# A pruned matrix product on one core: other places for the first loads, one transpose in a product bank, and another opening order on TensorE

## The chip, the core and the metric

The kernel runs on one core of a Trainium2 chip. Its engines run side by side, each with its own queue of instructions: TensorE (PE; its weight loads are shown as PEld), VectorE (DVE), ScalarE (ACT), GpSimd (POOL) and SyncE (SP), which here only issues transfers. ScalarE issues transfers too. The metric is device time in microseconds, the median of several runs.

## The reference

`x` is 16 x 512 x 1024, `w` 1024 x 1024 and `b` 1024 long, all bf16. Of every four neighbouring rows of `w`, in every column, the two of largest magnitude are kept; then a plain product and the bias:

```python
wg = w.reshape(G, M, D)                      # M = 4, G = D // 4
mag = jnp.abs(wg)
order = jnp.argsort(mag, 1)
thr = jnp.take_along_axis(mag, order[:, M - N:M - N + 1, :], 1)   # N = 2
mask = (mag >= thr).astype(w.dtype)
wp = (wg * mask).reshape(D, D)
return jnp.einsum("bsd,df->bsf", x, wp) + b
```

## The kernel before

The 8192 rows of `x` are 64 tiles of 128. From tile 12 on the kernel is a steady stream: a batch of tiles is loaded transposed by DMA (line 377), each tile takes 16 matmuls 512 wide against the pruned weights (line 239), and DVE adds the bias while it empties PSUM (line 400). All that matters here is the opening, in which the weights are still being loaded and pruned.

**Loads** (lines 110 to 124). `w` comes in pieces, the first 256 columns of its upper half in four DMAs that alternate between SyncE and ScalarE. `load_x` brings the left half of `x` for tiles 0 to 7. Each engine issues its DMAs in the order in which they are written. ScalarE's only other work at that point is a small activation (line 116), which has its table loaded.

**Pruning** (class Piece, lines 143 to 180). Six pieces of `w` are pruned one after the other, 0 to 3 of the upper half, 4 and 5 of the lower. For piece i the steps are abs, hi, lo, t1, t2, thr, mask and mult. DVE does all of them but one: the magnitudes of piece 3 (`abs3`) are made on ScalarE (line 157). Piece 0 has its mask and mult in four quarters u, v, s, t (one of the four rows of a group each), piece 1 in two halves x and y. The pruned rows stand in an interleaved order in `wp`; four DMAs a half ("W" tokens, line 141) spread them in natural order into `wp_nat`.

**Tiles 0 to 7** are multiplied in that interleaved order while pieces 0 to 3 come in. A tile t has its left half transposed by four matmuls with the identity ("T", line 189) into a bank of PSUM, and ScalarE copies it to SBUF ("C", line 194). Products "Mt.i" with a letter take the quarter or half of piece i (line 216, 256 columns, one matmul for each of the four rows of a group). Two tiles share a bank: the pairs are (5, 6), (0, 1), (2, 3), (4, 7), numbered 0 to 3. When a pair's products for a 256-column strip n are all done, ScalarE copies the bank to SBUF ("Sqbn", line 256: pair q, strip n), which frees it. So S2b0 waits for all products of piece 0 of tiles 2 and 3.

**Tiles 8 to 11** come transposed by DMA ("X" tokens, line 224); tokens "Ajhn" open their sums with the upper half (line 239), and lines 432 to 433 close them, then those of tiles 0 to 7, whose right half comes by the "Y" tokens (line 231). POOL adds the bias to the staged sums.

PSUM has eight banks: two in the pool `psum_t` (transposes, later tile 11) and six in `psum_o` (everything else, the fillers first). A tile of a pool gets a bank when the one that had it has been read.

**The order of the work is written out by hand**: lists of tokens for PE, DVE, ACT and SP (lines 258 to 280). `run` emits them engine by engine, a token as soon as what `needs` names for it has been emitted, and `seq` (line 64) ties each engine's instructions to that order. Fillers (line 133: 6 wide, 8 and then, as token F8, 8 narrow matmuls of constants) occupy TensorE while the first loads are under way. A transpose needs the copy of the one two before it, since `psum_t` has two banks.

In the order before, T7a, T5a and T6a stand first on TensorE, then products and transposes in turn, and all 32 products of piece 0 (8 tiles, u, v, s, t) precede the first of piece 1. ScalarE's list has the eight copies, S3b0, S0b0, S1b0, S2b0, then `abs3`, then further stage copies. Two of the four spreading DMAs of the lower half (W1.0q) are issued by ScalarE ahead of S3b3 and S0b3.

Of the kernel before, what the change touches and what calls it, by code (L numbers as in the profile page):

```python
# [10 lines left out]
def kernel(  # L11
# [8 lines left out]
    P = 128  # L20
    bf16 = mybir.dt.bfloat16
    fp32 = mybir.dt.float32
# [10 lines left out]
    FH = 512  # L33
# [24 lines left out]
    psum_t = ctx.enter_context(tc.tile_pool(name="psum_t", bufs=2, space=bass.MemoryType.PSUM))  # L58
    psum_o = ctx.enter_context(tc.tile_pool(name="psum_o", bufs=6, space=bass.MemoryType.PSUM))
# [10 lines left out]
    def pe(i):  # L70
        return seq("pe", i)
# [4 lines left out]
    def act(i):  # L76
        return seq("act", i)
# [13 lines left out]
    def tokens(dram, t):  # L91
        a, b_ = next(s for s in GROUPS if s[0] <= t < s[1])
        return dram[a * P:b_ * P].rearrange("(p t) k -> p t k", p=P), t - a
    bias_sb = const.tile([P, Dout], bf16)

    def issue(eng, out_, in_):
        q = nc.sync if eng == "sp" else nc.scalar
        return seq(eng, q.dma_start(out_, in_))  # L98

    def load_w(g, c0, c1, ma=0, mb=4, eng="sp"):  # L100
        issue(eng, w_sb[:, g, ma:mb, c0:c1], wv[:, g, ma:mb, c0:c1])

    def load_x(ta, tb, eng="sp"):
        xs = const.tile([P, tb - ta, HK], bf16, name=f"x_{ta}")
        xv, n = tokens(xf, ta)
        issue(eng, xs[:], xv[:, n:n + tb - ta, :HK])
        for t in range(ta, tb):
            x_sb[t] = xs[:, t - ta, :]
# [2 lines left out]
    load_w(0, 0, 256, 1, 2, "act")  # L111
    load_w(0, 0, 256, 2, 3)
    load_w(0, 0, 256, 3, 4, "act")
    load_x(7, 8, "act")
    load_x(0, 2, "act")
    act(nc.scalar.activation(spark[:], nc.const_aps.tensor(1.0, [P, 1], bf16), Act.Abs))
    load_x(5, 7)
    load_w(0, 256, 512)
    load_x(4, 5)
    load_x(2, 4)  # L120
    load_w(0, 512, 1024)
    load_w(1, 0, 512)
# [8 lines left out]
    def filler(n, rep=1):  # L131
        for _ in range(n):
            pe(nc.tensor.matmul(warm_ps[:, :rep * P], lhsT=nc.const_aps.tensor(1.0, [P, P], bf16),  # L133
                                rhs=nc.const_aps.tensor(1.0, [P, rep * P], bf16), start=True, stop=True))
# [4 lines left out]
    def spread(g, c0, c1, ks=range(4), eng="sp"):  # L139
        for k in ks:  # L140
            issue(eng, wp_nat[:, 4 * g + k, c0:c1], wp[32 * k:32 * k + 32, g, :, c0:c1])
# [41 lines left out]

    def transpose(t):
        xg = x_sb[t].rearrange("p (q m) -> p m q", m=4)
        bank = psum_t.tile([P, FH], fp32, name="tp")
        tp = bank[:].bitcast(bf16)[:, :FH].rearrange("p (m q) -> p m q", m=4)
        for m in range(4):
            pe(nc.tensor.transpose(tp[:, m, :], xg[:, m, :], ident[:]))  # L189
        xpk[t] = tp  # L190

    def copy_xt(t):
        xt = xtp.tile([P, 4, P], bf16, name="xt")
        act(nc.scalar.copy(xt[:].bitcast(fp32), xpk[t].bitcast(fp32)))  # L194
        xpk[t] = xt
# [27 lines left out]
    def load_lead(g):  # L223
        sp(nc.sync.dma_start_transpose(out=xlead[:, 4 * g:4 * g + 4, :],
                                       in_=xf[NPK * P:(NPK + LEAD) * P, g * HK:(g + 1) * HK]))
        return {NPK + j: xlead[:, :, j * P:(j + 1) * P] for j in range(LEAD)}

    def load_low(u):
        a, b_ = GROUPS[u]
        xlow = const.tile([P, 4, (b_ - a) * P], bf16, name=f"xlow{u}")  # L230
        sp(nc.sync.dma_start_transpose(out=xlow[:], in_=xf[a * P:b_ * P, HK:]))
        xq = xlow[:].rearrange("p k (q t) -> p k q t", t=b_ - a)
        return {a + t: xq[:, :, :, t] for t in range(b_ - a)}
# [8 lines left out]
    def open_nat(j, h):  # L242
        t = NPK + j
        if j < 3:
            held[(t, h)] = psum_o.tile([P, FH], fp32, name="ps")
        else:
            held[(t, h)] = psum_t.tile([P, FH], fp32, name="tp")
        nat(xnat[t], held[(t, h)][:], h * FH, (h + 1) * FH, 0, 4)
# [3 lines left out]
    def stage(q, n):  # L252
        if (q, n // 2) not in staged:
            staged[(q, n // 2)] = stg.tile([P, 2, 2, CW], fp32, name="st")
        st = staged[(q, n // 2)]
        act(nc.scalar.copy(st[:, n % 2, :, :].rearrange("p t c -> p (t c)"), ps_open.pop((q, n))[:]))  # L256

    order = {
        "pe": (
            "F8 T7a T5a T6a M7.0u M5.0u T1a M7.0v M5.0v M6.0u M6.0v T0a M7.0s M5.0s M6.0s M7.0t M5.0t M6.0t "  # L260
            "T4a M1.0u M1.0v M1.0s M1.0t T3a M0.0u M0.0v M0.0s M0.0t T2a M4.0u M4.0v M4.0s M4.0t "
            "M3.0u M3.0v M3.0s M3.0t M2.0u M2.0v M2.0s M2.0t M4.1x M5.1x M0.1x M7.1y M6.1y M2.1y M1.1y "
            "M3.1y M6.1x M4.1y M1.1x M3.1x M0.1y M7.1x M2.1x M5.1y M0.2 M3.2 M7.2 M1.2 M2.2 M4.2 "
            "M6.2 M0.3 M2.3 M5.3 M4.3 M5.2 M6.3 M3.3 M1.3 A0h0 A2h0 M7.3 A2h1 A1h0 A3h1 A0h1 A3h0 "
            "A1h1"
        ),
        "dve": (
            "abs0a hi0a abs0b lo0a lo0b hi0b t20 t10 thr0 mask0u mask0v mult0u mult0v mask0s mask0t mult0s mult0t abs1 lo1 hi1 "
# [2 lines left out]
            "thr5 mask5 mult5"  # L271
        ),
        "act": (
            "C7a C5a C6a C1a C0a C4a C3a C2a S3b0 S0b0 S1b0 S2b0 abs3 S3b1 S1b1 S0b1 S2b1 S2b2 S1b2 "
            "S3b2 S0b2 S1b3 S2b3 W1.0q S3b3 S0b3"
        ),
        "sp": (
# [9 lines left out]
    def all_of(tok, i):  # L287
        return [tok + x for x in halves.get(i, ("",))]

    def split_tok(tok):  # L290
        k = tok[-1] if tok[-1] in "xyabuvst" else ""
        return (tok[:-1] if k else tok), k

    transposed = []

    def needs(eng, tok):
        base, k = split_tok(tok)
        if tok[0] == "C":
            return ["T" + tok[1:]]
        if tok[0] == "T":  # L300
            return ["C" + transposed[-2]] if len(transposed) > 1 else []
        if tok[0] == "F":
            return []
        if tok[0] == "W":
            g, h = map(int, tok[1:4].split("."))
            return [n for i, pc in enumerate(pieces) if pc[0] == g and pc[1] // FH == h for n in all_of(f"mult{i}", i)]
        if tok[0] in "XY":
            return []
        if tok[0] == "A":
            return ["X0", f"W0.{tok.split('h')[1]}"]  # L310
        if base[0] == "M":
            t, i = base[1:].split(".")
            return [f"C{t}a", f"mult{i}{k}"]
        if tok[0] == "S":
            q, n = map(int, tok[1:].split("b"))
            return [f"M{t}.{x}" for i, pc in enumerate(pieces) if pc[0] == 0 and pc[1] // CW == n
                    for t in pairs[q] for x in all_of(str(i), i)]
        i, step = base[-1], base[:-1]
        before = {"abs": [], "hi": ["abs"], "lo": ["abs"], "t1": ["hi"], "t2": ["lo"],
                  "thr": ["t1", "t2"], "mask": ["thr", "hi", "lo"], "mult": ["mask"]}[step]  # L320
        out_ = []
        for b_ in before:
            if b_ in ("abs", "hi", "lo") and int(i) in by_rows:
                out_ += [b_ + i + k] if step in ("hi", "lo") else [b_ + i + s for s in "ab"]
            else:
                out_.append(b_ + i + (k if b_ == "mask" else ""))
        return out_

    def emit(eng, tok):
        base, k = split_tok(tok)  # L330
        if tok[0] == "T":
            transpose(int(tok[1:-1]))
            transposed.append(tok[1:])
        elif tok[0] == "F":
            filler(int(tok[1:]))
        elif tok[0] == "W":
            g, h = map(int, tok[1:4].split("."))
            spread(g, h * FH, (h + 1) * FH, {"": range(4), "p": range(2), "q": range(2, 4)}[tok[4:]], eng)
        elif tok[0] == "X":
            xnat.update(load_lead(int(tok[1:])))  # L340
        elif tok[0] == "Y":
            xnat.update(load_low(int(tok[1:])))
        elif tok[0] == "A":
            open_nat(*map(int, tok[1:].split("h")))
        elif tok[0] == "C":
            copy_xt(int(tok[1:-1]))
        elif tok[0] == "M":
            mm_piece(*map(int, base[1:].split(".")), part[k])
        elif tok[0] == "S":
            stage(*map(int, tok[1:].split("b")))  # L350
        else:
            i = int(base[-1])
            if i not in p:
                p[i] = Piece(i)
            if eng == "act":
                p[i].abs_act()
            else:
                p[i].do(base[:-1], part[k], half.get(k, slice(0, 2)))
# [78 lines left out]
    for bi, (tb, nb) in enumerate(batches):  # L437
        if bi:
            load_batch(bi + 1)
        for j in range(nb):  # L440
            t = tb + j
            xt = xnat[t]
            o = outp.tile([P, Dout], bf16, name="o")
            if t == NT - 1:
                for n, (c0, c1) in enumerate(((0, FH), (FH, FH + CW), (FH + CW, Dout - P), (Dout - P, Dout))):
                    ps = psum_o.tile([P, FH], fp32, name="ps")
# [44 lines left out]
```

## Time and profile before

| what | value |
|---|---|
| time, median of 3 runs | 233.24 us (233.21 to 233.59) |
| the profiled execution's own time | 233.31 us |
| its span | 231.5 us |
| first weights read by DVE (abs0a) | starts at 3.10 us |
| first transpose on TensorE | starts at 5.28 us |
| S3b0 to S2b0, first strip's stage copies | 10.31 to 12.36 us |
| abs3 on ScalarE | 12.23, 1.09 long |
| first sums of tiles 8 to 11 open | 21.03 us |
| mult5, the last step of pruning | ends at 27.66 us |
| first batch of the steady stream | TensorE from 49.1 us |

Times in the traces count from the start of the span. A line of the timeline gives start, length, engine, line of the kernel, operation, what is written from what, and in brackets how long the engine stood before it and what released it. A matmul's length includes the way through the array, so matmuls overlap; the distance between starts is what each costs in a stream.

### The profile page before, as it was taken

Reading aid. Unit: us, or ns where it says so; the run is one execution under the profiler, and the core shown is the slowest. Engines: PE = TensorE matmul, PEld = TensorE weight load, DVE = VectorE, ACT = ScalarE, POOL = GpSimd, SP = SyncE. Lnnn points to the kernel's source line nnn. Section 1 sums busy time; section 2 is a strip of 40 time slices with the busy share of each in tenths; the row PEclk is TensorE's granted clock in tenths of the full one; section 3 lists DMA queues with packets and bytes.
Section 4 is the critical chain, followed back from the end, with each engine's and each line's share of the span. In section 5 each row is a group of like instructions: output and inputs, shape, how many; then the busy total and the mean of one; then the engine's idle time right before and its main releaser. Section 6 shows DMA issues by size and latency. Waiting matters only on the chain.

```text
span 231.5 us, 2851 instructions
## 1 busy us (share of the span) xinstructions
PE 227.7 (98%) x1158; PEld 112.6 (49%) x1158; DVE 107.8 (47%) x188; ACT 13.7 (6%) x27; POOL 17.6 (8%) x15
## 2 busy tenths in 40 slices
PE   8999999999999999999999999999999999999995
PEld 5887444544444444444444444444444444444443
DVE  4999778754334324324424424424424423423434
ACT  2774100000000000000000000000000000000000
POOL 1000299700000000000000000000000000000000
DMA  6999989997299222992249921795129962122122
GB/s 198 358 216 223 223 179 256 271 258 273 94 231 262 99 91 63 224 272 80 88 119 224 246 93 59 163 283 151 73 91 181 226 182 82 57 91 86 57 87 91
DMA packets 78268, 38.19 MB, mean 165 GB/s; under 512 B 63664, under 2 KB 70576, under 8 KB 78256
## 3 DMA queue, kind: packets, MB, share of 16 engines
q1 hardware_dynamic: 67328, 20.61, 44.1%
q10 hardware_dynamic: 10928, 17.40, 21.5%
q8 instruction: 9, 0.15, 0.3%
q14 instruction: 3, 0.02, 0.0%
HBM read 3.41 MB, written 16.78 MB: 87 GB/s over the span
## 4 chain that ended last, share of the span: by engine, by line
PE 96%; DMA 2%; ACTq 0%; ACT 0%; DVE 0%; issue 0%
PE ps L239 88%; PE ps L216 6%; DMA x<-in_x_dram 2%; PE tp L239 1%; PE tp L189 1%; ACTq L98 0%; ACT xt L194 0%; DVE o L400 0%
## 5 line engine op out<-in xcount | busy, mean ns | idle before, releaser
L239 PE MATMUL ps<-wp_nat,xb 128*128 128x512 bf16 (+2 forms) x848 | 179.8, 375 | 0.0
L239 PEld LDWEIGHTS <-xb 128*128 128x128 bf16 x848 | 82.4, 98 | 97.5
L400 DVE TENSOR_TENSOR o<-ps,bias_sb 128x512 bf16<-128x512 f32 (+1 forms) x112 | 71.6, 677 | 114.4 <-PE ps L239 114.3
L396 POOL TENSOR_TENSOR st<-st,bias_sb 128x1024 f32<-128x1024 f32 x8 | 16.8, 2131 | 0.0
L216 PE MATMUL ps<-wp,xt 128*128 128x256 bf16 x128 | 15.1, 273 | 0.0
L239 PE MATMUL ps<-wp_nat,xlow 128*128 128x512 bf16 x64 | 14.1, 379 | 0.0
L216 PEld LDWEIGHTS <-xt 128*128 128x128 bf16 x128 | 12.2, 98 | 1.6
L402 DVE TENSOR_TENSOR o<-ps,st 128x512 bf16<-128x512 f32 x16 | 11.1, 692 | 2.8 <-PE ps L239 2.3
L239 PE MATMUL ps<-wp_nat,xlead 128*128 128x512 bf16 x48 | 11.2, 379 | 0.0
L239 PEld LDWEIGHTS <-xlow 128*128 128x128 bf16 x64 | 7.2, 112 | 6.7
L239 PEld LDWEIGHTS <-xlead 128*128 128x128 bf16 x64 | 6.2, 98 | 7.1
L256 ACT COPY st<-ps 128x512 f32<-128x512 f32 x16 | 8.4, 595 | 6.0 <-PE ps L216 3.7
L154 DVE TENSOR_TENSOR mag<-mag,hi 128x256 bf16<-128x256 bf16 (+3 forms) x10 | 5.6, 582 | 0.2
L154 DVE TENSOR_TENSOR wp<-w_sb,mag 128x256 bf16<-128x256 bf16 (+3 forms) x10 | 5.6, 580 | 0.1
L133 PE MATMUL ps<-const-bfloat16-1.0 128*128 128x128 bf16 (+1 forms) x22 | 4.4, 395 | 0.8 <-PEq L475 0.8
L164 DVE TENSOR_SCALAR mag<-w_sb 128x512 uint16<-128x512 uint16 (+2 forms) x6 | 2.7, 466 | 3.1 <-DMA w_sb<-in_w_dram 3.1
L239 PE MATMUL tp<-wp_nat,xlead 128*128 128x512 bf16 x16 | 4.1, 379 | 0.0
L133 PEld LDWEIGHTS <-const-bfloat16-1.0 128*128 128x128 bf16 x22 | 2.5, 143 | 2.4 <-issue 2.4
L189 PE MATMUL tp<-ident,x 128*128 128x128 bf16 x32 | 3.0, 220 | 0.3 <-ACT xt L194 0.2
L154 DVE TENSOR_TENSOR hi<-mag 128x512 bf16<-128x512 bf16 (+2 forms) x7 | 3.2, 459 | 0.1
L154 DVE TENSOR_TENSOR lo<-mag 128x512 bf16<-128x512 bf16 (+2 forms) x7 | 3.1, 457 | 0.0
L194 ACT COPY xt<-tp 128x256 f32<-128x256 f32 x8 | 2.9, 374 | 3.2 <-PE tp L189 3.1
(15 smaller groups left out, 13.5 us busy)
## 6 DMA issues: line engine op xcount, KB each, us to landing
out_dram<-o ACTq DMA_DIRECT2D x59, 256.0 KB, 2.9
wp_nat<-wp SPq DMA_DIRECT2D x14, 128.0 KB, 3.4
w_sb<-in_w_dram SPq DMA_DIRECT2D x3, 512.0 KB, 6.3
out_dram<-o ACTq DMA_DIRECT2D x8, 128.0 KB, 1.7
x<-in_x_dram SPq DMA_DIRECT2D x2, 256.0 KB, 3.9
w_sb<-in_w_dram SPq DMA_DIRECT2D x1, 256.0 KB, 4.8
x<-in_x_dram ACTq DMA_DIRECT2D x1, 256.0 KB, 3.8
bias_sb<-in_b_dram SPq DMA_DIRECT2D x1, 256.0 KB, 6.4
```

Source lines behind the costliest of these rows:

```text
L133: pe(nc.tensor.matmul(warm_ps[:, :rep * P], lhsT=nc.const_aps.tensor(1.0, [P, P], bf16), rhs=nc.const_aps.tensor(1.0, [P, rep * P], bf16), ...
L154: dve(nc.vector.tensor_tensor(out, a, b_, op=op))
L164: dve(nc.vector.tensor_single_scalar(self.mag[:, ms, :].bitcast(u16), self.w[:, ms, :].bitcast(u16), 0x7FFF, op=Alu.bitwise_and))
L189: pe(nc.tensor.transpose(tp[:, m, :], xg[:, m, :], ident[:]))
L194: act(nc.scalar.copy(xt[:].bitcast(fp32), xpk[t].bitcast(fp32)))
L216: pe(nc.tensor.matmul(ps[:, c0 + d:c1 + d], lhsT=xpk[t][:, m, :], rhs=wp[:, g, m, c0:c1], start=(new and m == ms.start), stop=(left[(q, n) ...
L239: pe(nc.tensor.matmul(ps, lhsT=xt[:, kt - koff, :], rhs=wp_nat[:, kt, c0:c1], start=(kt == first), stop=(kt == last)))
L256: act(nc.scalar.copy(st[:, n % 2, :, :].rearrange("p t c -> p (t c)"), ps_open.pop((q, n))[:]))
L396: pool(nc.gpsimd.tensor_tensor(st[:], st[:], bias[:, :, None, :].to_broadcast([P, 2, 2, CW]), op=Alu.add))
L400: dve(nc.vector.tensor_tensor(o[:, c0:c1], ps, bias_sb[:, c0:c1], op=Alu.add))
L402: dve(nc.vector.tensor_tensor(o[:, c0:c1].rearrange("p (n c) -> p n c", n=2), ps.rearrange("p (n c) -> p n c", n=2), add, op=Alu.add))
```

## The change

Three things, and nothing else:

- The loads: tiles 5-6 and tile 4 are issued by ScalarE, third and fourth on it, in place of tile 7 and tiles 0-1. Tile 7 is third on SyncE in place of tiles 5-6. Tiles 0-1 come on SyncE behind the second weights, in place of tile 4.
- T6a writes to a bank of `psum_o` and not of `psum_t`. It has no copy to wait for and is not counted among the transposes that later ones wait for.
- The order: T4a comes fourth and C4a fourth. The products of piece 0 are in another order, and M2.0t, the last of them, stands behind eight tokens (sixteen matmuls) of piece 1.

```diff
-    load_x(7, 8, "act")
-    load_x(0, 2, "act")
+    load_x(5, 7, "act")
+    load_x(4, 5, "act")
     act(nc.scalar.activation(spark[:], nc.const_aps.tensor(1.0, [P, 1], bf16), Act.Abs))
-    load_x(5, 7)
+    load_x(7, 8)
     load_w(0, 256, 512)
-    load_x(4, 5)
+    load_x(0, 2)
     load_x(2, 4)
...
-        bank = psum_t.tile([P, FH], fp32, name="tp")
+        bank = psum_o.tile([P, FH], fp32, name="ps") if t == 6 else psum_t.tile([P, FH], fp32, name="tp")
...
         "pe": (
-            "F8 T7a T5a T6a M7.0u M5.0u T1a M7.0v M5.0v M6.0u M6.0v T0a M7.0s M5.0s M6.0s M7.0t M5.0t M6.0t "
-            "T4a M1.0u M1.0v M1.0s M1.0t T3a M0.0u M0.0v M0.0s M0.0t T2a M4.0u M4.0v M4.0s M4.0t "
-            "M3.0u M3.0v M3.0s M3.0t M2.0u M2.0v M2.0s M2.0t M4.1x M5.1x M0.1x M7.1y M6.1y M2.1y M1.1y "
-            "M3.1y M6.1x M4.1y M1.1x M3.1x M0.1y M7.1x M2.1x M5.1y M0.2 M3.2 M7.2 M1.2 M2.2 M4.2 "
-            "M6.2 M0.3 M2.3 M5.3 M4.3 M5.2 M6.3 M3.3 M1.3 A0h0 A2h0 M7.3 A2h1 A1h0 A3h1 A0h1 A3h0 "
-            "A1h1"
+            "F8 T7a T5a T6a M7.0u T4a M7.0v M5.0u M5.0v M6.0v M6.0u M6.0s M5.0t M4.0u M5.0s M4.0s M7.0s "
+            "T1a M7.0t M6.0t M4.0v T0a M4.0t M1.0u T3a M1.0v M1.0t M0.0v M0.0t T2a M0.0s M1.0s M0.0u "
+            "M3.0u M3.0t M3.0s M2.0u M3.0v M2.0v M2.0s M7.1y M5.1x M6.1y M0.1x M4.1x M2.1y M6.1x M4.1y "
+            "M2.0t M1.1x M1.1y M3.1x M3.1y M0.1y M7.1x M2.1x M5.1y M0.2 M3.2 M7.2 M1.2 M2.2 M4.2 M6.2 "
+            "M0.3 M2.3 M5.3 M4.3 M5.2 M6.3 M3.3 M1.3 A0h0 A2h0 M7.3 A2h1 A1h0 A3h1 A0h1 A3h0 A1h1"
         ),
...
-            "C7a C5a C6a C1a C0a C4a C3a C2a S3b0 S0b0 S1b0 S2b0 abs3 S3b1 S1b1 S0b1 S2b1 S2b2 S1b2 "
+            "C7a C5a C6a C4a C1a C0a C3a C2a S3b0 S0b0 S1b0 S2b0 abs3 S3b1 S1b1 S0b1 S2b1 S2b2 S1b2 "
...
         if tok[0] == "T":
-            return ["C" + transposed[-2]] if len(transposed) > 1 else []
+            return ["C" + transposed[-2]] if tok != "T6a" and len(transposed) > 1 else []
...
             transpose(int(tok[1:-1]))
-            transposed.append(tok[1:])
+            if tok != "T6a":
+                transposed.append(tok[1:])
```

## The prediction

> **What bounds the kernel now.** I read the page's first part, then the chain of waits in order of time, then the waits of TensorE, then timelines of single engines.
>
> ```profile
> PE 227.7 (98%) x1158; PEld 112.6 (49%) x1158; DVE 107.8 (47%) x188; ACT 13.7 (6%) x27; POOL 17.6 (8%) x15
> ```
>
> TensorE is busy for 227.7 of 231.5 us. Its work is not changed in number or size, so the change can only win or lose where TensorE stands still. The chain in order of time (start, length, what) shows where that is:
>
> ```profile
> 1.66 3.57 DMA x<-in_x_dram
> 5.24 0.05 issue
> 5.28 0.43 PE tp L189 x4
> 5.71 0.02 issue
> 5.73 0.38 ACT xt L194
> 6.11 0.04 issue
> 6.16 0.38 PE tp L189 x4
> ...
> 9.84 11.35 PE ps L216 x104
> ```
>
> and the waits of TensorE in the first 60 us (who for whom, total, times, longest):
>
> ```profile
> PE ps L133 <- PEq L475: 0.8, 1, 0.8
> PE tp L189 <- ACT xt L194: 0.2, 1, 0.2
> ```
>
> Tile 7 lands at 5.24 and its transposes start at 5.28; the fillers' weight loads end at 4.93 (3.29 + 1.64 in the timeline), so 0.35 us pass there. T6a then waits for C7a: eight transposes at 0.055 each would end at 5.72, T6a starts at 6.16, 0.44 lost. After 6.16 no wait is listed; the products run at 0.109 each and the last matmul ends the kernel. **So the opening holds at most 0.35 + 0.44 = 0.79 us, 0.34% of 233.24.**
>
> The other side is how near TensorE's suppliers run behind it. Timelines of ACT, DVE and PE, in that order of fences (start, us, engine, line, op, idle before):
>
> ```profile
> 9.88 0.37 ACT L194 COPY xt<-tp 128x256 f32<-128x256 f32 x1 [0.29 <-PE tp L189]
> 10.31 2.05 ACT L256 COPY st<-ps 128x512 f32<-128x512 f32 x4
> 12.23 1.09 ACT L157 ACTIVATE mag<-w_sb 128x1024 bf16<-128x1024 bf16 x1
> ...
> 22.84 1.67 ACTq L98 DMA_DIRECT2D wp_nat<-wp  x2
> 24.55 1.07 ACT L256 COPY st<-ps 128x512 f32<-128x512 f32 x2 [2.25 <-DVE hi L154]
> ```
>
> ```profile
> 12.96 0.69 DVE L154 TENSOR_TENSOR wp<-w_sb,mag 128x1024 bf16<-128x1024 bf16 x1
> 13.57 0.41 DVE L154 TENSOR_TENSOR hi<-mag 128x512 bf16<-128x512 bf16 x1
> ```
>
> ```profile
> 24.92 1.03 PE L239 MATMUL tp<-wp_nat,xlead 128*128 128x512 bf16 x4
> 25.78 1.03 PE L239 MATMUL ps<-wp_nat,xlead 128*128 128x512 bf16 x4
> ```
>
> The reader is to see: S3b0 to S2b0 and then abs3 follow each other on ScalarE; abs3 ends at 13.32, only 0.25 before DVE's hi3 at 13.57. DVE has no gap from 3.10 to 27.66, so what is late at hi3 is late in mult3, mult4 and mult5. W1.0q (22.84) waits for mult4 and holds S3b3 (24.55) and S0b3 behind it on ScalarE; those free the banks of A0h1 (25.78) and A1h1 (27.51).
>
> **Part 1, loads.** The same bytes are moved in the same eight first DMAs, so nothing is added or removed. Tile 7 takes the place (SyncE, third, issued at 1.65) in which tiles 5-6, twice its bytes, landed at 1.65 + 3.3 = 4.95; it is there by then, and the start is set by the fillers, 4.93 to 4.95. Tiles 5-6 take ScalarE's third place: tile 7 landed from it at 5.24, tiles 0-1 from the fourth at 2.15 + 3.8 = 5.95. Both are bounds; as the queue has moved 128 KB less than for the second, I take 5.3. Tile 4 comes fourth there, with the same bytes ahead and including it as tiles 0-1 had: 5.95, wanted at 6.16. Tiles 0-1 are issued at 3.10: tile 4 landed from there at 7.2, tiles 2-3 from the next place at 8.0; both queues together have asked for 1,280 KB by its end as they had by tile 4's, so 7.2 to 7.4, wanted at 7.6. The second weights are behind 128 KB less, and DVE is busy until 6.92 anyway: no gain. Bias and the last weights go out behind as before. Four issues stand on ScalarE ahead of its table load in both versions, so that moves nothing.
>
> The Trainium skill, DMA: Bandwidth & Descriptors, section Issuing engines are not separate DMA queues, speaks against this part: loads of either engine run on the same 16 DMA engines, and a second queue saves only issue time. This trace does not quite agree: 256 KB from SyncE landed 0.3 us before 128 KB from ScalarE, issued within 0.02 us. By the rule alone tile 7 would land at 5.24 as now, and the time would be 0.1 us longer than the sum below.
>
> **Part 2, T6a in a product bank.** T7a, T5a and T6a no longer wait for a copy: from 4.95, 0.22 for each, T5a and T6a from 5.3, so they end at 5.74. M7.0u needs C7a and mult0u. C7a: tile 7's transposes to copy 0.45, copy 0.37, to TensorE 0.05 (6.10 to 6.16): 4.95 + 0.87 = 5.82. mult0u: 5.71 + 0.28 + 0.05 = 6.04, the later. Before, M7.0u stood at 6.38 with the same 12 transposes done. Gain 6.38 - 6.05 = 0.33. In the new order M5.0t then meets mult0t (6.72 + 0.28 + 0.05 = 7.06, wanted at 7.04), 0.02 lost, and no other copy or mult is late by more: M7.1y is wanted at 10.88 - 0.31 = 10.57, mult1y is there at 9.92 + 0.42 + 0.05 = 10.39. **So the gain g is 0.30.** Its lower end is -0.05 (tiles 5-6 only at 5.95: M7.0u at 6.42); the upper end 0.33. T6a's bank is one more allocation of psum_o, but it is also one more bank already free, so every later bank waits for the same copy as before.
>
> The clock: the fillers still step at 0.107 us at 4.89, the transposes at 0.055 from 5.37, so the faster step came between. Twelve transposes at 0.107 from 4.95 would end at 6.23 and take 0.18 of g away.
>
> The Trainium skill, TensorE: Matmul & The Clock Gate, section Part 1: The HAM clock gate, says the switch follows about 3.4 us of work and, its window running freely, can shift by 0.5 us. No run here shows the shift; four products of 0.109 at half speed would make the time 0.4 us longer by it.
>
> **Part 3, new opening order.** M2.0t, the last product of S2b0's bank, moves from the 32nd product to the 48th. Before, the 33rd stands at 9.68 + 12 x 0.109 = 10.99, so the 48th at 12.63 - g. ScalarE's copy starts 0.31 after its last product (M4.0t at 9.68 + 3 x 0.109 = 10.01, S3b0 at 10.31): S2b0 at 12.94 - g. Behind it on the same engine stands abs3, one copy pitch later ((12.23 - 10.31) / 4 = 0.48): 13.42 - g, ending 1.09 later at 14.51 - g, and hi3 can start at 14.56 - g where it stood at 13.57. **DVE is 0.99 - g = 0.69 us late from hi3 on.** What covers that, each cover less 0.99 since TensorE itself comes g earlier:
> - mult3 at 16.50 + 0.05, M0.3 wants it at 17.54: 0.99 of cover, just met.
> - W1.0: its last piece landed at 23.52 + 4.0 = 27.5, wanted by (8,0)'s last matmul at 29.02: 1.5, enough. W1.1: 33.7 against 35.06: 1.35, enough. Y0 behind W1.0p on SyncE lands at 31.5, wanted at 40.2.
> - W1.0q on ScalarE: S3b3 at 24.55 + 0.59 + 0.05 = 25.19, A0h1 at 25.78: **0.59 only. TensorE stands 0.99 - 0.59 = 0.40 us before A0h1.** S0b3 is wanted at 27.51 and ends at 25.63: 1.88, enough.
>
> That S3b3 and not S0b3 frees A0h1's bank I infer: both A0h1 and A1h1 wait for ScalarE again, which the second would not need if the first had waited for the later copy. The second DMA of W1.0q took 1.00 us to issue, its first 0.64; most wp_nat issues take 0.60. If 0.36 of it belongs to a transfer that no longer overlaps it, the stall is 0.04. I take its own row, 1.00.
>
> **Sum** against the profiled execution (span 231.5, 233.31 with what lies around it, 0.07 above the median 233.24): -0.30 + 0.40 = +0.10, so 233.34 from the median; its own range 232.95 to 233.6. After A0h1 no wait is listed up to the end, and the batch loads land 10 us or more before use (for the second batch 52.5 against 62.9), so this stays to the end.
>
> **Rivals.**
> 1. The opening's gain arrives whole: W1.0q's second issue takes 0.64 and the stall vanishes. For it: 13 of 16 such issues are at 0.64 or less. Against: this one's own row. 233.24 - 0.30 = 232.94.
> 2. Slower: A0h1 takes the bank that S0b3 frees. Its cover is 25.78 - 25.68 = 0.10, so TensorE stands 0.99 - 0.10 = 0.89 there: +0.59, 233.83. For it: q0's last bank was opened (M5.3) before q3's (M4.3), and a plain rotation would give it out first. Against: A1h1's own wait. The same price comes if the second issue is 1.57 long, as one of W1.1's was. It decides from a stall of 0.77 on.
> 3. The opening gives nothing, tiles 5-6 landing at 5.95: g = -0.05, the stall unchanged at 0.99 - 0.59: 233.24 + 0.05 + 0.40 = 233.69.
> 4. More than the 0.47 us of 0.2% is won: the opening's 0.79 would have to come almost whole, but mult0u at 6.04 stands in the way, unless DVE's first weights land earlier. 232.7.
>
> **How the numbers follow.** Forecast 0.42, rival 1 0.17, rival 2 0.23, rival 3 0.10, rival 4 0.08. A measurement of this kernel can tell about 0.2% (0.47 us) from no change. Forecast, rival 1 and rival 3 lie within it but for their edges: 0.02 of rival 1 is faster, 0.04 of rival 3 slower. Faster 0.10, slower 0.27, same 0.63. The range goes from rival 1 to rival 2: 232.9 to 233.85.
>
> **What would show it.** Tile 7's transposes at 4.95 and T6a without a gap; M7.0u near 6.05. S2b0 alone near 12.65 with ScalarE idle ahead of it, abs3 near 13.1; DVE idle 0.7 us ahead of hi3, released by ScalarE's line 157; TensorE idle near 25.5 for 0.4 us, released by line 256. No gap on DVE at hi3 would overturn part 3; a gap of TensorE elsewhere, above all ahead of T5a, T1a, M0.3 or (8,0), would make the prediction wrong in its working.

## The result and the profile after

The changed kernel takes 233.73 us (median of 22 runs, 233.13 to 234.21), the kernel before 233.35 us beside it (22 runs, 233.07 to 233.62). The ratio is 1.0014, 95% interval 1.0008 to 1.0021: slower by 0.33 us, 0.19 to 0.49. The prediction was 233.34, net +0.10; its range, 232.9 to 233.85, holds the time, but +0.10 lies below the interval of the difference. The profiled execution took 234.21 us, the highest of the 22, with a span of 232.4, so it shows the loss larger than the median has it.

The page's first part, the changed kernel:

```profile
PE 227.5 (98%) x1158; PEld 112.0 (48%) x1158; DVE 108.0 (46%) x188; ACT 13.5 (6%) x27; POOL 17.6 (8%) x15
```

TensorE's busy time is that of before within 0.2; the 0.9 us of span are idle time. The chain of waits in order of time (start, length, what) says where:

```profile
3.02 5.49 DMA x<-in_x_dram
8.51 0.05 issue
8.55 0.41 PE tp L189 x4
...
10.62 2.96 PE ps L216 x27
...
13.61 0.59 ACT st L256
14.19 0.97 ACT mag L157
...
15.18 0.42 DVE hi L154
...
23.21 1.22 DVE wp L154
...
25.14 0.88 ACTq L98
...
26.06 0.59 ACT st L256
...
26.69 1.02 PE ps L239 x4
```

Before, the chain ran through TensorE alone from 6.16 on. Now it begins with a load of `x` that lands at 8.51 and starts T1a (8.55). It runs through M2.0t into S2b0 (13.61) and abs3 (14.19), then through sixteen steps of VectorE from hi3 (15.18) to mult4 (23.21), W1.0q on ScalarE and S3b3 (26.06), and comes back to TensorE at A0h1, 26.69 where before had 25.78: 0.91 later. TensorE's timeline splits the 0.91:

```profile
25.59 1.03 PE L239 MATMUL tp<-wp_nat,xlead 128*128 128x512 bf16 x4
26.69 1.02 PE L239 MATMUL ps<-wp_nat,xlead 128*128 128x512 bf16 x4
```

A3h1, the group just ahead, starts at 25.59 where before had 24.92. So 0.67 was lost earlier, and 0.24 is the wait at A0h1 itself (26.69 less 25.59, less the 0.86 that the four matmuls of A3h1 take). The waits of the first 60 us, the same kernel:

```profile
PE tp L189 <- DMA x<-in_x_dram: 0.9, 1, 0.9
...
DVE hi L154 <- ACT mag L157: 0.8, 1, 0.8
PE ps L216 <- DVE wp L154: 0.6, 1, 0.6
```

The first is T1a, the second hi3, the third M7.0u on mult0u. The first transposes and T1a in TensorE's timeline:

```profile
4.56 0.62 PE L189 MATMUL tp<-ident,x 128*128 128x128 bf16 x8
5.01 0.39 PE L189 MATMUL ps<-ident,x 128*128 128x128 bf16 x4
5.97 0.27 PE L216 MATMUL ps<-wp,xt 128*128 128x256 bf16 x1 [0.56 <-DVE wp L154]
...
6.29 1.39 PE L216 MATMUL ps<-wp,xt 128*128 128x256 bf16 x11
8.55 0.41 PE L189 MATMUL tp<-ident,x 128*128 128x128 bf16 x4 [0.87 <-DMA x<-in_x_dram]
```

T7a starts at 4.56, 0.72 earlier than before, T6a follows with no gap, M7.0u starts at 5.97 where it stood at 6.38: the opening did what it was to do, 0.41 won there. The last of the eleven products ahead of T1a starts at 7.41 and takes 0.109 in the stream, so T1a starts 1.04 after TensorE was free (the bracket's 0.87 counts from that product's end): all of the 0.41 is lost again, and 0.63 more.

A second place where the two traces differ is the queue of SyncE's loads. What SyncE's queue (q1) and ScalarE's (q10) moved from 3.7 to 4.7 us (packets, MB, share of the DMA engines), before:

```profile
q10 hardware_dynamic: 250, 0.24, 77.3%
q1 hardware_dynamic: 111, 0.10, 29.9%
```

and after:

```profile
q10 hardware_dynamic: 289, 0.27, 90.5%
q1 hardware_dynamic: 12, 0.01, 9.2%
```

With tile 7 done (4.34), SyncE's queue is as good as empty for much of that microsecond although the second weights had been issued at 2.11 and 2.12. Their first packets move at 4.44 where before had 4.71, and from 4.7 to 7.2 the queue moves 0.73 MB in either kernel: having less ahead of them gains them little. Whether this hole is what made tiles 0-1 late is taken up after the experiments.

### The profile page after: what moved, and what is told of

It reads as the page before. It is cut to its first block, busy times and chain, and to the rows that moved or that the text cites. A ratio compares the mean times of both kernels' runs of the same rounds, so it can differ in the third digit from the quotient of the medians.

```text
span 232.4 us, 2851 instructions
## 1 busy us (share of the span) xinstructions
PE 227.5 (98%) x1158; PEld 112.0 (48%) x1158; DVE 108.0 (46%) x188; ACT 13.5 (6%) x27; POOL 17.6 (8%) x15
## 4 chain that ended last, share of the span: by engine, by line
PE 90%; DVE 4%; DMA 3%; ACT 1%; ACTq 0%; issue 0%
PE ps L239 86%; DMA x<-in_x_dram 2%; PE ps L216 2%; DVE hi L154 1%; PE tp L239 1%; DMA w_sb<-in_w_dram 1%; DVE mag L154 1%; DVE wp L154 1%; DVE lo L154 1%; DVE mag L164 1%; ACT st L256 1%; PE tp L189 0%; ACT mag L157 0%; ACTq L98 0%; DVE o L400 0%
## 5 line engine op out<-in xcount | busy, mean ns | idle before, releaser
L133 PE MATMUL ps<-const-bfloat16-1.0 128*128 128x128 bf16 (+1 forms) x22 | 3.9, 357 | 0.8 <-PEq L475 0.8
L189 PEld LDWEIGHTS <-x 128*128 128x128 bf16 x32 | 2.3, 114 | 1.6 <-DMA x<-in_x_dram 1.2
```

## The experiments

Two theories. **O, the order**: M2.0t's late place holds S2b0, abs3 behind it, hi3, the pruning, W1.0q, S3b3 and at last A0h1. **L, the landing**: the loss is made at T1a by tiles 0-1. "Ratio" is that of the runs to the runs of the kernel before on the same chip, with its 95% interval.

**The changed kernel again.**

> The changed kernel once more, for a second profile beside the slow one that was shown. Theory O (the order): ScalarE stands behind S2b0 for M2.0t, so hi3 on VectorE waits for abs3 and TensorE waits ahead of A0h1; net 0.40 us minus g, where g is how much earlier than before M2.0t's 48th place is reached. Theory L (the landing): the loss is made ahead of T1a, where tiles 0-1 land late behind the second weights on SyncE. Both expect about 233.7 us (0.4 over the kernel before) and tiles 0-1 landed between 7.5 and 8.5; O expects a wait at hi3 and ahead of A0h1 here too, whatever T1a waits; L alone expects the end to be late by just the wait at T1a less the 0.3 won in the opening.

233.74 us against 233.34, ratio 1.0012 (1.0000 to 1.0024). Tiles 0-1 landed at 8.33 and T1a started at 8.37, 0.87 after TensorE was free; hi3 started at 15.00 and A0h1 at 26.51 after a wait of 0.24. Both waits are there, as O expects. A0h1 is 0.73 late (26.51 for 25.78): 0.49 of it was there at A3h1 (25.41 for 24.92), 0.24 is the wait. So both theories have a share in this execution, and the next runs take one or the other away.

**abs3 ahead of S2b0.**

```diff
-  S1b0 S2b0 abs3 S3b1
+  S1b0 abs3 S2b0 S3b1
```

> abs3 stands ahead of S2b0 in ScalarE's list, all else as changed. O: hi3 has no wait, TensorE none ahead of A0h1; the time is the kernel before's minus g, with g near 0 by the median of the changed kernel, so about 233.35 us, 0.4 less than the changed kernel. L: T1a still waits and the end is as late as it was, about 233.7.

233.34 us against 233.34, ratio 0.9999 (0.9986 to 1.0012). ScalarE's timeline:

```profile
11.82 1.09 ACT L157 ACTIVATE mag<-w_sb 128x1024 bf16<-128x1024 bf16 x1
13.07 0.59 ACT L256 COPY st<-ps 128x512 f32<-128x512 f32 x1 [0.16 <-PE ps L216]
```

abs3 is done at 12.91, S2b0 now waits for M2.0t alone and nobody behind it minds. No wait of hi3 and none of A0h1 is listed. O said 233.35, L 233.7. TensorE's chain runs through to the end without leaving it, as before. In this execution, however, tiles 0-1 had landed at 7.34 and T1a (8.04) waited for nothing, so its profile doesn't tell O from L; the medians do, but weakly, since this interval and the changed kernel's (1.0000 to 1.0024) overlap.

**M2.0t back in its place.**

```diff
-  M2.0s M7.1y ... M4.1y M2.0t M1.1x
+  M2.0s M2.0t M7.1y ... M4.1y M1.1x
```

> M2.0t stands ahead of M7.1y again, directly behind M2.0s; loads, bank and the rest as changed. O: S2b0 follows S1b0 at once, hi3 has no wait by ScalarE, no wait ahead of A0h1; about 233.35 us, as with abs3 ahead of S2b0. L: no difference to the changed kernel, 233.7.

233.08 us against 233.34, ratio 0.9996 (0.9980 to 1.0011). S2b0 follows S1b0, hi3 and A0h1 wait for nothing. That is what O expects, but tiles 0-1 had landed early here too (7.14); and whether anything is won is open.

> The changed kernel with M2.0t ahead of M7.1y, once more, since its first median (233.08) was 0.26 under the kernel before with an interval that reaches to both sides. If it is the gain of the opening that O lets through, it stays at 233.0 to 233.15; if it was chance, it is 233.3 like the kernel with abs3 moved.

233.53 us against 233.59, ratio 0.9988 (0.9963 to 1.0013). Neither answer can be told from this: it is no slower than before, and the interval reaches over a gain of 0.3 and over none. Its profile does separate the theories: tiles 0-1 landed at 7.98 and T1a started at 8.03, 0.39 after TensorE was free, yet hi3 and A0h1 waited for nothing (A0h1 at 25.93, 0.14 late). With the order mended, the wait at T1a is what is left.

**M2.0t still later.**

```diff
-  M4.1y M2.0t M1.1x M1.1y M3.1x M3.1y M0.1y
+  M4.1y M1.1x M1.1y M3.1x M3.1y M2.0t M0.1y
```

> The changed kernel with M2.0t another four tokens later, behind M3.1y: eight matmuls of 0.109, 0.87 us. O prices M2.0t's place one to one: S2b0, abs3, hi3 and A0h1 each 0.87 later, the time 0.87 over the changed kernel, 1.25 over the kernel before, 234.6 us; part of the wait of TensorE moves up to M0.3, since mult3 has no cover left there. L: the same as the changed kernel, 0.4 over the kernel before.

234.61 us against 233.61, ratio 1.0053 (1.0034 to 1.0073). O's price was 0.87 over the changed kernel; by the ratios it is 0.91 (1.0053 less 1.0014, times 233.6). L said no difference. The wait that the prediction had seen coming once mult3's cover is used up is there as well, TensorE's timeline of this kernel:

```profile
15.92 2.35 PE L216 MATMUL ps<-wp,xt 128*128 128x256 bf16 x20 [0.36 <-ACT st L256]
18.43 0.83 PE L216 MATMUL ps<-wp,xt 128*128 128x256 bf16 x6 [0.16 <-DVE wp L154]
```

The second is M0.3 on mult3. The first I had left out: M7.2, which was released at 15.88 by the end of S3b1 (15.29), the copy right behind abs3 on ScalarE. The trace prices M2.0t's place more closely than the times do: A0h1 starts 19.02 after T1a here (26.95 less 7.93) and 18.14 after it in both profiles of the changed kernel, 0.88 more for the 0.87 that O had said.

**S3b3 ahead of W1.0q.**

```diff
-  S1b3 S2b3 W1.0q S3b3 S0b3
+  S1b3 S2b3 S3b3 W1.0q S0b3
```

> The changed kernel with S3b3 ahead of W1.0q on ScalarE, so that only S0b3 stands behind those two DMAs; hi3 stays late. If S3b3 frees A0h1's bank, as the prediction inferred, the wait of 0.24 ahead of A0h1 is gone; W1.0q starts about 0.3 later and lands about 29.4, so up to 0.2 can come back ahead of (8,0)'s last matmul: 0.1 to 0.3 under the changed kernel. If S0b3 frees it, the wait at A0h1 stays and grows by about 0.3. If the loss is all made at T1a (L), the time is that of the changed kernel.

233.54 us against 233.61, ratio 0.9994 (0.9985 to 1.0004); by the ratios 0.47 under the changed kernel, more than the 0.1 to 0.3 expected, but the two intervals come within 0.1 of each other, so the size is loose. ScalarE and then TensorE:

```profile
23.83 0.59 ACT L256 COPY st<-ps 128x512 f32<-128x512 f32 x1 [1.09 <-PE ps L216]
24.22 1.56 ACTq L98 DMA_DIRECT2D wp_nat<-wp  x2
25.82 0.59 ACT L256 COPY st<-ps 128x512 f32<-128x512 f32 x1 [1.41 <-DVE hi L154]
```

```profile
25.35 1.03 PE L239 MATMUL tp<-wp_nat,xlead 128*128 128x512 bf16 x4
26.22 1.03 PE L239 MATMUL ps<-wp_nat,xlead 128*128 128x512 bf16 x4
```

A0h1 (26.22) starts 0.87 after A3h1 (25.35), four matmuls, with no wait, while S0b3 only starts at 25.82 and ends at 26.41. So S3b3 frees A0h1's bank; rival 2's first reading falls. hi3 still waited 1.07 for abs3 in this execution and A0h1 didn't notice: here VectorE's delay reached TensorE through S3b3 alone. A0h1 is still 0.44 later than before (26.22 for 25.78), which TensorE brought along from the opening: T1a started at 8.31, with tiles 0-1 landed at 8.27.

**The loads as before, the rest as changed.**

```diff
-    load_x(5, 7, "act") ; load_x(4, 5, "act") ; ... ; load_x(7, 8) ; load_w(0, 256, 512) ; load_x(0, 2)
+    load_x(7, 8, "act") ; load_x(0, 2, "act") ; ... ; load_x(5, 7) ; load_w(0, 256, 512) ; load_x(4, 5)
```

> The loads as before (tile 7 and tiles 0-1 on ScalarE, 5-6 and 4 on SyncE), the bank of T6a and the order as changed. L: T1a has its tiles by 6.0, the loss is gone and the opening's gain stays, about 0.2 below the kernel before: 233.1 us. O: g is 0.22 (T7a at 5.28, M7.0u at 6.16), hi3 still 0.77 late, wait ahead of A0h1 0.40: net 0.18 over the kernel before, 233.5 us. Tile 4 lands on SyncE near 7.2 there and T4a wants it at 6.3; if that wait of 0.9 comes, both are later by up to 0.9.

234.63 us against 233.34, ratio 1.0056 (1.0041 to 1.0070). The waits:

```profile
DVE hi L154 <- ACT mag L157: 1.7, 1, 1.7
...
PE tp L189 <- DMA x<-in_x_dram: 1.0, 1, 1.0
```

Tile 4 landed at 7.21 and T4a waited for it, as the expectation had allowed; the new order needs the new loads. It is a miss as a test of L, but a good one of O: with M2.0t 0.79 late by T4a (13.73 - 0.31 for 12.63), S2b0 started at 13.73, hi3 at 15.31 and A0h1 at 26.82, 1.04 late. Tiles 0-1 were there at 6.11 and T1a waited for nothing, and A0h1 still waited 0.24.

**The new loads alone, in the kernel before.**

```diff
-    load_x(7, 8, "act") ; load_x(0, 2, "act") ; ... ; load_x(5, 7) ; load_w(0, 256, 512) ; load_x(4, 5)
+    load_x(5, 7, "act") ; load_x(4, 5, "act") ; ... ; load_x(7, 8) ; load_w(0, 256, 512) ; load_x(0, 2)
```

> The kernel before with the changed loads alone; transposes, banks and order as before. T1a is the fourth transpose there and is wanted near 6.2 to 6.6, tiles 0-1 land at 7.2 to 8.5 behind the second weights: TensorE waits 0.7 to 1.9 us at T1a. M2.0t is before the products of piece 1, so theory O gives no wait at hi3 unless T1a's wait makes one: M2.0t at 10.9 plus 1.3, S2b0 12.5, abs3 to 14.0, hi3 0.5 late. Time 0.6 to 1.5 over the kernel before: 234.0 to 234.9. If the landing were no matter (tiles 0-1 there by 6.2) it would be 233.1.

234.84 us against 233.59, ratio 1.0042 (1.0009 to 1.0075). Tiles 0-1 landed at 7.96 and T1a waited 1.5. So the landing is real, and its price is set by when the order wants T1a. (This profile is of an execution of 236.31 us in which TensorE's clock dropped after that wait; see the last section.)

**The bank of T6a alone, in the kernel before.**

```diff
-    bank = psum_t.tile(..., name="tp")
+    bank = psum_o.tile(..., name="ps") if t == 6 else psum_t.tile(..., name="tp")
...
```

The lines that take T6a out of the transposes' waits go with it, as in the change.

> The kernel before with T6a's bank from the product pool alone; loads and order as before. T6a follows T5a without a gap and M7.0u starts at its copy or mult, 6.05 to 6.16 for 6.38: 0.2 to 0.3 won if nothing takes it. S2b0 moves with TensorE, hi3 has no wait, A0h1 a cover of 0.59: 233.1 us. If T1a, which is next, then waits for its copy in the smaller bank pool, the gain is lost there: 233.35.

233.77 us against 233.59, ratio 1.0009 (0.9980 to 1.0039): inconclusive, since the interval spans 1.4 us. In its profiled execution tile 7 itself landed at 6.24 and T7a started at 6.29, which hides what the bank may win.

**Both waits out of the way.** Tiles 0-1 in ScalarE's fourth place, tiles 1, 0, 4 in the places of 4, 1, 0, and abs3 first:

```diff
-    load_x(4, 5, "act")
+    load_x(0, 2, "act")
...
-    load_x(0, 2)
+    load_x(4, 5)
...
-  T6a M7.0u T4a ... M4.0u M5.0s M4.0s M7.0s T1a M7.0t M6.0t M4.0v T0a M4.0t M1.0u T3a
-  M1.0v M1.0t M0.0v M0.0t T2a M0.0s M1.0s M0.0u
+  T6a M7.0u T1a ... M1.0u M5.0s M1.0s M7.0s T0a M7.0t M6.0t M1.0v T4a M1.0t M0.0u T3a
+  M0.0v M0.0t M4.0v M4.0t T2a M4.0s M0.0s M4.0u
...
-  C7a C5a C6a C4a C1a C0a C3a C2a S3b0 S0b0 S1b0 S2b0 abs3
+  C7a C5a C6a C1a C0a C4a C3a C2a S0b0 S1b0 S3b0 abs3 S2b0
```

> Changed kernel with tiles 0-1 fourth on ScalarE again, tile 4 behind the second weights, tiles 1, 0, 4 in the places of 4, 1, 0 in the opening order, and abs3 ahead of S2b0. Tiles 0-1 land by 6.0 and T1a wants them near 6.2; tile 4 lands at 7.2 to 8.0 and is wanted near 8.1: no wait of TensorE for a load, none at hi3, none ahead of A0h1. If the late landings of tiles 0-1 cost the changed kernel part of its time beside O, this is below the kernel with abs3 moved alone, 233.0 against 233.34; if they cost nothing there, the two are equal.

233.36 us against 233.59, ratio 0.9992 (0.9961 to 1.0023): the interval reaches to both sides. Tile 7 landed at 5.38 in its profile and T7a started at 5.42.

> The mix once more (tiles 0-1 fourth on ScalarE, tiles 1, 0, 4 in the places of 4, 1, 0, abs3 ahead of S2b0), on another chip time, beside the kernel before. First ratio 0.9992, interval 0.9961 to 1.0023. If the opening's gain is real once both waits are out of the way, it is 0.1 to 0.3 under the kernel before again; if the start of the first transposes eats it, it equals it.

233.06 us against 233.61, ratio 0.9986 (0.9974 to 0.9998): faster than the kernel before by 0.33 us, 0.05 to 0.61, the one version whose interval lies under it, in one of two measurements. TensorE's timeline in its second profile:

```profile
4.71 0.61 PE L189 MATMUL tp<-ident,x 128*128 128x128 bf16 x8
5.16 0.39 PE L189 MATMUL ps<-ident,x 128*128 128x128 bf16 x4
5.97 0.27 PE L216 MATMUL ps<-wp,xt 128*128 128x256 bf16 x1 [0.43 <-DVE wp L154]
6.08 0.38 PE L189 MATMUL tp<-ident,x 128*128 128x128 bf16 x4
6.30 1.39 PE L216 MATMUL ps<-wp,xt 128*128 128x256 bf16 x11
```

Tiles 0-1 landed at 5.75, the fourth transpose has them at 6.08, and after mult0u TensorE stands for nothing: A0h1 at 25.40, 0.38 earlier than before.

**The rod from S2b0 to A0h1.** Across the executions in which ScalarE held abs3 behind a late M2.0t, these starts were read from the timelines (us):

| kernel | S2b0 | hi3 | hi3 - S2b0 | A0h1 | A0h1 - hi3 |
|---|---|---|---|---|---|
| changed | 13.61 | 15.18 | 1.57 | 26.69 | 11.51 |
| changed, again | 13.43 | 15.00 | 1.57 | 26.51 | 11.51 |
| old loads | 13.73 | 15.31 | 1.58 | 26.82 | 11.51 |
| M2.0t later | 13.85 | 15.43 | 1.57 | 26.95 | 11.52 |
| S3b3 first | 13.37 | 14.94 | 1.57 | 26.22 | 11.28, no wait |

The prediction had 1.62 (0.48 + 1.09 + 0.05) and 11.62 (25.19 less 13.57). However late S2b0 was, and whatever made it late, A0h1 came 13.08 to 13.10 after it, until S3b3 was taken out of the way.

## Why the prediction was right, and what it missed

The time fell inside the range, and the path on which the change loses is the one that the prediction described. The net is not: +0.38 by the medians for +0.10. Two sizes were off, in opposite directions: the wait at A0h1 is 0.24 where 0.40 was said, and g, said to be 0.30, is about -0.14. That the first error hides part of the second is luck.

**Part 3, right in mechanism, its price 0.16 too high.** hi3 released by abs3 behind S2b0, TensorE released ahead of A0h1 by the stage copy: each stood in the trace where it was said to be. The price was 0.40 - g. The table makes it 0.24 - g: M2.0t at 12.63 - g, the copy 0.31 later, A0h1 13.08 after that, is 26.02 - g for 25.78. The 0.16 between them are 0.12 of the second issue of W1.0q, which took 0.88 and not 1.00 (25.14 in the chain) and so lay between the two bounds given, nearer the one taken, and 0.04 of small latencies. Moving abs3 gave back 0.40 by the medians (233.34 for 233.74 on the same chip time) and 0.30 by the ratios, with intervals too wide to tell that from 0.24.

**Part 2, right up to M7.0u.** T6a without a gap, M7.0u set by mult0u: 5.97 where 6.05 was said, and 5.95 in the second profile. In three other profiles with this opening TensorE's first steps took twice as long and M7.0u came at 6.27 to 6.40, which is the risk that the prediction's paragraph on the clock had named. The version that keeps the opening and drops both waits is 0.33 faster by the ratio of its second measurement, with A0h1 0.38 earlier in the profile; that agrees with the 0.30 said of g where no load is late, but it is one execution and a wide interval.

**Part 1, the step that was mis-sized: "both queues together have asked for 1,280 KB by its end as they had by tile 4's, so 7.2 to 7.4, wanted at 7.6".** Tiles 0-1 landed at 8.51, 8.33, 7.34, 7.14, 7.96, 7.98, 7.88 and 8.27 in the eight profiled executions with these loads: twice as said, six times 0.5 to 1.1 past 7.4. The landing of a load is reported in sixteen parts, and most of them came as counted: by 7.40 there were 14, 13, 16, 16, 8, 14, 14 and 13 of the sixteen. In the two profiles of the changed kernel fifteen parts had landed at 7.71 and 7.80, the last at 8.51 and 8.33. So the count of bytes had no term for the last parts; why they straggle the runs don't show.

The hole in SyncE's queue doesn't tell the late ones from the others. It stands in all eight executions (0.01 to 0.05 MB in that microsecond, before 0.10), also in the two that landed as said (0.02 and 0.04), where ScalarE's queue moved 0.34 and 0.31 MB in place of 0.24. In the changed kernel's first profile both queues together moved 0.28 MB for 0.34, so a small part may come of it there. Nor is the straggling shown to come of the new loads: with the loads of the kernel before, tile 4 in the same place landed at 7.23, 7.21 and, in the run with the bank alone, 8.37. (The second weights, on the same queue, landed at 7.67 in the changed kernel's first profile and VectorE stood 0.77 for them; that is hidden, since hi3 waits for abs3 anyway.) Tile 7 at 4.34 and tiles 5-6 at 4.71 in that profile were as early as said or earlier; tile 4 (5.30) was no matter.

So g, given as 0.30 with a lower end of -0.05, was below that end in the profiled execution. S2b0 there at 13.61 is M2.0t at 13.30 for 12.63: g = -0.67, and 0.24 + 0.67 = 0.91, the measured lateness of A0h1. In the other profiles with M2.0t in that place g is -0.49 (changed, again), -0.13 (abs3 first) and -0.43 (S3b3 first). T1a's wait for tiles 0-1 cost 1.04, 0.87, nothing and 0.21 in these four; in the last two TensorE's first steps, twice as long, took the gain. For the median's +0.38, g is about -0.14 by the same sum; that one is inferred, not read. The loss counts in full, since TensorE comes that much later to everything behind T1a; the order adds the 0.24 at A0h1.

**The rivals.** Rival 1 (no stall at A0h1, the opening's gain whole) did not come: the issue took 0.88 and not 0.64, and the versions with abs3 or M2.0t moved have no stall but no clear gain either. Rival 2's bank is ruled out by the run with S3b3 first, though its time lies only 0.10 above the median. Rival 3 (the opening gives nothing) came near the truth in its number, 233.69 for 233.73, with the wrong transfer, not tiles 5-6 but tiles 0-1, and with a stall of 0.40 for 0.24: in part luck. Rival 4 never showed in a median.

**The clock** was named as a risk of 0.18 and is real, in either direction: in the changed kernel's profile the fillers sped up early and T7a started at 4.56 for the 4.95 said, with abs3 first M7.0u came at 6.28 for 6.05. It is told below.

## What to carry to other kernels

When a product is moved down an engine's order, look for who reads its last result, and then for what stands behind that reader on its own engine: here one 0.1 us matmul, moved past sixteen others, delayed an unrelated piece of pruning and came back 13 us later through a bank. Such a delay is a rod: it has one length, and it can be cut at any joint (abs3 ahead of S2b0, S3b3 ahead of W1.0q, M2.0t in its place); abs3 and S2b0 don't even need each other. And a landing is better forecast as a range read from several traces: the bytes counted over the queues gave 7.2 to 7.4 here, which most parts of the load met, but its reader waits for the last part, and that came between 7.14 and 8.51.

## What was not expected of the hardware

**The switch of TensorE's clock moves from execution to execution.** All kernels begin with the same fillers from 0.77 on. In the changed kernel eight transposes started at 4.56 and the next at 5.01, 0.056 each; with abs3 first:

```profile
5.00 1.06 PE L189 MATMUL tp<-ident,x 128*128 128x128 bf16 x8
5.85 0.63 PE L189 MATMUL ps<-ident,x 128*128 128x128 bf16 x4
```

eight steps in 0.85, 0.106 each. The profile's clock column has 1.00 there all the same, so the switch is read from the steps; where the column has 0.50, in the run below, the steps are the same (T0a's four from 9.28, the next product at 9.70).

The Trainium skill, TensorE: Matmul & The Clock Gate, section Part 1: The HAM clock gate, gives about 3.4 us of work and a shift of 0.5 us; the traces agree that it shifts, but the first fast step seen lay between 4.0 and 6.8 us in thirteen profiles, 3.3 to 6.0 after the first filler, so the shift is wider than the page has it.

**After a long wait in the opening the clock was halved once.** In the kernel with the new loads alone TensorE waited 1.5 us for tiles 0-1; the stretch with that wait and the one after it (behind the busy times of PE, PEld, DVE, ACT and POOL stand PEclk, the share of the DMA engines and GB/s):

```profile
4.00:8.00 4.00, 2.38 (x26) 1.69 (x23) 3.73 (x16) 1.28 (x4) 0.00 (x0) 0.99 0.93 294
8.00:11.00 3.00, 2.99 (x19) 2.33 (x20) 2.91 (x10) 0.74 (x2) 0.00 (x0) 0.50 1.09 371
```

The granted clock was 0.50 for three microseconds, with products 0.21 apart in place of 0.109; that execution ended 1.5 us above its kernel's median. The changed kernel's wait of 0.87 at T1a had no such row. That the wait caused it isn't shown: two of the 35 runs of the kernel before beside it have the same mean clock, 0.993, and were not profiled.

**Landings scatter far more than compute.** The same load in the same place of the same queue landed between 7.14 and 8.51, while the way from S2b0 to A0h1 came out the same to 0.02 in four executions. The scatter is more than the whole effect of the change. It may be why the changed kernel's runs spread over 1.1 us in the main comparison, where those of the kernel before spread over 0.6; that is not shown, and beside the next four runs the kernel before spread over 1.1 as well.
